# Transposing normalised activations on TensorE instead of by DMA, with part of a broadcast moved and the instruction order redone

## Chip, cores, metric

One core of a Trainium2 chip. The metric is the device time in microseconds of one execution. Several executions are taken in each job, and the kernel before runs beside every kernel that is tried, on the same chip. Engines are named as in the profile: PE (TensorE), PEld (its weight loads), DVE (VectorE), ACT (ScalarE), POOL (GpSimd), SP (the queue that issues DMAs).

## The reference

Four residual layers A, B, A, B on one sequence of 2048 tokens with 512 features and 32 heads of 16.

```
x = x + A(layernorm(x)); x = x + B(layernorm(x)); x = x + A(...); x = x + B(...)

A (linear attention):  q,k,v = x @ wqkv;  pq = q @ w_phi, pk = k @ w_phi  (per head)
    phi = [softmax(p), softmax(-p)]
    kv = sum over tokens phi_k v,  z = sum over tokens phi_k
    o  = (phi_q kv) / (phi_q z + 1e-6);  out = o @ wo

B (local attention):   8 keys at distance 0, 2, .., 14;  softmax(q k / 4);  out = (attn v) @ wo
```

Layer A sums over all keys before any query is answered. That is the one barrier in each pair of layers. The kernel works on four blocks of 512 tokens.

## The kernel before

The instruction stream of each engine follows a fixed list of steps (`_ORDER`, some 1,400 entries of two characters, made in advance). Each entry runs one step of one stage on one engine, and PE, DVE, ACT and SP keep the order in which the list emits them.

The norm makes `xn` on DVE, and one DMA per block transposes it, so that features lie on the partitions:

```python
def s_norm(self, st, key, b, T, op0, scale):
    # ... ln(): reciprocal standard deviation on ACT
    def ap(t):                       # DVE, four times 128 tokens
        if t == 0:
            T["xn"] = self.med([4, D], "xn")
        nc.vector.tensor_scalar(out=T["xn"][:, t, :], in0=self.x[b][:, t, :], ...)

    def tr():                        # SP
        xnT = self.med([4, NB, P], "xnT")
        nc.sync.dma_start_transpose(out=xnT[:].rearrange("k t c p -> k (t c) p"),
                                    in_=T["xn"][:].rearrange("p t d -> p (t d)"))
        self.xnT[key, b] = xnT
    add(st, "ACT", ln)
    for t in range(4):
        add(st, "DVE", ap, t)
    add(st, "SP", tr)
```

There are 16 such norms: four blocks ahead of each layer. In layer A the normaliser `rho` (one number for head and token) is spread over the features in one of two ways:

```python
# s_a3, after md (PE), dr (DVE), ln (ACT), rho (DVE)
for s in range(2):
    if dma:                          # blocks 1, 2, 3 of each layer
        add(st, "SP", wr, s)         # rho to DRAM
        add(st, "SP", rdb, s)        # read back 16-fold, 512 KB
        add(st, "DVE", muld, s)      # one product of 2048 columns
    else:                            # block 0
        add(st, "PE", bc, s)         # 16 small products with a 0/1 matrix, into four PSUM banks
        for t in range(4):
            add(st, "DVE", mulp, s, t)   # four products of 512 columns, from PSUM
```

Layer B writes V of a block to DRAM (`vd`) and reads it back shifted (`Vg`, 8 DMAs of 260 KB). DVE then multiplies queries with keys (`prod`) and weights with values (`pav`), in instructions of 2.3 us. At the start comes a check of the column norms of two folded weights.

At the start a check of the column norms of two folded weights squares them on POOL:

```python
def sq(qk):
    w = self.WA[:, :, qk * D:(qk + 1) * D]
    nc.gpsimd.tensor_tensor(out=T[qk][:], in0=w, in1=w, op=ALU.mult)
```

Of the kernel before, what the change touches and what calls it, by code (L numbers as in the profile page):

```python
# [8 lines left out]
BF16 = mybir.dt.bfloat16  # L9
# [3 lines left out]
ACT = mybir.ActivationFunctionType  # L13
# [10 lines left out]
NB = 4  # L24
# [11 lines left out]
SUM_R_MAX = 1e10  # L36
DEN_TINY = 2.0 ** -60

_OPT = {"rho_dma": (1, 2, 3), "pe_resid": {}}

_E = mybir.EngineType
_ORDERED = {_E.PE, _E.DVE, _E.Activation, _E.SP}
# [42 lines left out]


class _Fast:
# [97 lines left out]
    def setup(self):  # L185
        nc, const = self.nc, self.const
        nc.scalar.preload_act_table_set("natural_log_exp_and_others")
        self.WA = const.tile([P, NB, 3 * D], BF16, name="WA")
        self.WoA = const.tile([P, NB, D], BF16, name="WoA")
        self.WB = const.tile([P, NB, 3, NB, P], BF16, name="WB")  # L190
        self.WoB = const.tile([P, NB, D], BF16, name="WoB")
        WA = self.WA
        self.wraw = self.big([NB, 2 * D], "wraw")
        wraw = self.wraw
        wav = self.A_wqkv.rearrange("(m p) c -> p m c", p=P)
        self.phis = self.t2([NB, DH], "phis")
# [108 lines left out]
    def s_norm(self, st, key, b, T, op0, scale):  # L305
        nc, add = self.nc, self.step
# [13 lines left out]
        def tr():  # L320
# [514 lines left out]
    def stages(self):  # L835
        for b in range(4):
            self.s_ln_first(b)
        self.s_fold(1)
        self.s_fold(0)
        self.s_load_B()  # L840
        for L in range(2):
            for b in range(4):
                self.s_a1(L, b)
            for b in range(4):
                self.s_a2(L, b)
            if L == 0:
# [73 lines left out]
class _Layout:  # L920
# [578 lines left out]
```

## Time and profile before

| | before |
|---|---|
| time, median (3 runs) | 425.43 us |
| span in the trace | 422.1 us |
| PE / DVE / ACT busy | 327.1 / 317.0 / 253.6 us |
| DVE idle | 105.1 us |

A busy figure is the time in which the engine had an instruction in work. PE's includes the time that the half clock adds. The prediction shows the page's lines, and it cuts the span in three at the first of the six small DVE instructions that take the finished sums of a layer A (called ZM). I use the same cut, I, II and III, throughout. These are the rows of the windows table of the kernel before for the three (us; then busy time of PE, PEld, DVE, ACT, POOL; granted clock; DMA share; GB/s):

```profile
0.00:74.50 74.50, 50.24 (x378) 29.11 (x383) 48.85 (x93) 42.72 (x89) 17.11 (x33) 0.93 0.47 114
74.50:267.70 193.20, 167.04 (x1351) 75.26 (x1361) 148.44 (x224) 139.97 (x314) 0.83 (x5) 0.94 0.48 95
267.70:422.10 154.40, 109.81 (x778) 43.01 (x779) 119.70 (x159) 70.92 (x156) 0.15 (x1) 0.85 0.54 119
```

### The profile page before, as it was taken

The page shows a single profiled execution, that of the slowest core. Times are in us where ns is not written, and L with a number is a line of the kernel's source. Part 1 is how long each engine was busy: PE and PEld are TensorE (multiplying, and loading weights), DVE is VectorE, ACT ScalarE, POOL GpSimd, SP SyncE. Part 2 cuts the span into 40 slices and gives each one's busy share as a digit, 9 for nine tenths or more (in the row PEclk, how much of TensorE's full clock was granted, in tenths as well). Part 3 has the DMA queues.
Part 4 walks back from the last instruction along what each step waited for, and adds up shares of the span by engine and source line. Part 5 has one row for each costly group of instructions (what it writes and reads, how often), then busy time and mean ns, then how long its engine had stood idle before and what let it go on. Part 6 is the DMA issues. An engine that isn't in the chain of part 4 may idle for free.

```text
span 422.1 us, 6496 instructions
## 1 busy us (share of the span) xinstructions
PE 327.1 (78%) x2499; PEld 147.4 (35%) x2521; DVE 317.0 (75%) x476; ACT 253.6 (60%) x559; POOL 18.1 (4%) x39
## 2 busy tenths in 40 slices
PE   0449989889999948942999999519899999671582
PEld 0414438534444313410344364503344433120131
DVE  2796937868529999795679983546879999866893
ACT  1318798688767564680889978506797666630220
POOL 2334200000000000000000000000000000000000
PEclk9959999999999977995899999857999999975598
DMA  8966000244872991399202020084055018799913
GB/s 261 331 109 101 0 2 2 57 107 64 159 184 80 210 190 28 101 206 203 47 2 50 0 51 2 9 209 103 10 92 99 2 50 193 169 195 219 225 59 108
DMA packets 68166, 45.24 MB, mean 107 GB/s; under 512 B 38304, under 2 KB 66464, under 8 KB 68128
## 3 DMA queue, kind: packets, MB, share of 16 engines
q1 hardware_dynamic: 66544, 43.69, 48.5%
q10 hardware_dynamic: 1584, 1.07, 0.8%
q8 instruction: 21, 0.34, 0.4%
q14 instruction: 17, 0.14, 0.1%
HBM read 29.64 MB, written 6.72 MB: 86 GB/s over the span
## 4 chain that ended last, share of the span: by engine, by line
PE 41%; DMA 24%; DVE 19%; ACT 10%; issue 2%; SPq 1%; ACTq 0%; DVEq 0%
PE ps L676 16%; DMA xnT<-xn 5%; PE ps L506 5%; PE ps L363 5%; PE ps L423 4%; DMA vd<-V 4%; DMA Prho<-rd 4%; DMA Vg<-vd 3%; DMA rd<-rho 3%; DVE x L376 3%; PE ps L478 3%; DVE xn L317 3%; ACT Eq L512 2%; DMA wraw<-in_A_wqkv_dram 2%; PE ps L435 2%
## 5 line engine op out<-in xcount | busy, mean ns | idle before, releaser
L676 PE MATMUL ps<-xnT,WB 128*128 128x512 bf16 x384 | 87.6, 384 | 4.2 <-DMA xnT<-xn 4.1
L794 DVE TENSOR_TENSOR pav<-PT,Vg 128x4096 bf16<-128x4096 bf16 x32 | 71.9, 2287 | 17.7 <-DMA Vg<-vd 8.9
L734 DVE TENSOR_TENSOR prod<-QT,K 128x4096 bf16<-128x4096 bf16 x32 | 71.4, 2285 | 3.1 <-ACT QT L690 1.6
L676 PEld LDWEIGHTS <-WB 128*128 128x128 bf16 x384 | 37.0, 99 | 53.6 <-issue 10.5
L376 DVE SCALAR_TENSOR_TENSOR x<-ps,x 128x512 bf16<-128x512 f32 x64 | 42.9, 684 | 10.6 <-PE ps L363 10.5
L506 PE MATMUL ps<-xnT,WA 128*128 128x512 bf16 x128 | 31.9, 400 | 13.8 <-DMA xnT<-xn 13.2
L807 ACT CAST oT<-ps 128x512 bf16<-128x512 f32 x32 | 18.4, 590 | 40.2 <-PE ps L801 40.2
L512 ACT ACTIVATE Eq<-ps 128x512 bf16<-128x512 f32 x64 | 34.0, 625 | 13.4 <-PE ps L506 13.4
L801 PE MATMUL ps<-pav,indAV 128*32 128x512 bf16 x256 | 22.6, 449 | 23.9 <-DVE pav L794 23.5
L389 ACT ACTIVATE sqd<-x,nmean 128x512 bf16<-128x512 bf16 x48 | 34.4, 719 | 9.1 <-DVE nmean L382 8.8
L363 PEld LDWEIGHTS <-oT 128*128 128x128 bf16 x256 | 24.3, 101 | 39.7 <-issue 8.8
L435 PE MATMUL ps<-WA,xnT 128*128 128x512 bf16 x123 | 30.4, 391 | 9.8 <-DMA xnT<-xn 9.4
L429 ACT ACTIVATE Ek<-ps 128x512 bf16<-128x512 f32 x64 | 32.9, 636 | 2.6 <-PE ps L423 2.6
L363 PE MATMUL ps<-WoB,oT 128*128 128x512 bf16 x124 | 32.6, 408 | 1.1 <-ACT oT L807 0.8
L363 PE MATMUL ps<-WoA,oT 128*128 128x512 bf16 x123 | 30.1, 380 | 2.1 <-ACT oT L658 1.4
L423 PE MATMUL ps<-WA,xnT 128*128 128x512 bf16 x122 | 29.0, 379 | 0.7 <-DVE WA L241 0.4
L690 ACT CAST QT<-ps 128x512 bf16<-128x512 f32 x32 | 18.7, 586 | 13.4 <-PE ps L676 13.4
L658 ACT CAST oT<-ps 128x512 bf16<-128x512 f32 x32 | 16.8, 597 | 14.1 <-PE ps L652 14.1
L449 DVE TENSOR_TENSOR s<-Ek 128x2048 bf16<-128x2048 bf16 x8 | 12.8, 1600 | 16.5 <-ACT Ek L429 16.5
L506 PEld LDWEIGHTS <-WA 128*128 128x128 bf16 x128 | 12.8, 102 | 30.9 <-DMA xnT<-xn 13.8
L652 PE MATMUL ps<-Eq,R 128*128 128x512 bf16 x64 | 17.6, 414 | 7.0 <-DVE Eq L627 6.9
L627 DVE TENSOR_TENSOR Eq<-Eq,Prho 128x2048 bf16<-128x2048 bf16 x12 | 14.6, 1222 | 11.2 <-DMA Prho<-rd 11.2
(103 smaller groups left out, 391.4 us busy)
## 6 DMA issues: line engine op xcount, KB each, us to landing
Vg<-vd SPq DMA_DIRECT2D x64, 260.0 KB, 8.1
Prho<-rd SPq DMA_DIRECT2D x12, 512.0 KB, 4.8
vd<-V SPq DMA_DIRECT2D x8, 512.0 KB, 3.3
x<-in_A_x_dram SPq DMA_DIRECT2D x4, 512.0 KB, 9.8
out_dram<-x SPq DMA_DIRECT2D x8, 256.0 KB, 2.2
wbraw<-in_B_wqkv_dram SPq DMA_DIRECT2D x3, 512.0 KB, 10.0
wraw<-in_A_wqkv_dram SPq DMA_DIRECT2D x1, 512.0 KB, 4.3
WA<-in_A_wqkv_dram ACTq DMA_DIRECT2D x1, 512.0 KB, 7.5
```

Source lines behind the costliest of these rows:

```text
L363: nc.tensor.matmul(y[:], lhsT=oT[:, c, t * P:(t + 1) * P], rhs=Wo()[:, c, :], start=(c == 0), stop=(c == NB - 1 and t not in pe_res))
L376: nc.vector.scalar_tensor_tensor(out=xb[:, t, :], in0=T[t][:], scalar=1.0, in1=xb[:, t, :], op0=ALU.mult, op1=ALU.add, **kw)
L389: nc.scalar.activation(out=sqd[:], in_=xb[:, t, :], func=ACT.Square, bias=T["nm"][:, t:t + 1], accum_out=T["ss"][:, t:t + 1])
L423: nc.tensor.matmul(pk[:], lhsT=xnT[:, t, k, :], rhs=self.WA[:, k, D:2 * D], start=(k == 0), stop=(k == NB - 1))
L429: nc.scalar.activation(out=T["E"][:, t, s, :], in_=T["k", t][:], func=ACT.Exp, scale=1.0 - 2.0 * s)
L435: nc.tensor.matmul(pv[:], lhsT=xnT[:, t, k, :], rhs=self.WA[:, k, 2 * D:3 * D], start=(k == 0), stop=(k == NB - 1))
L506: nc.tensor.matmul(pq[:], lhsT=self.WA[:, k, hb * P:(hb + 1) * P], rhs=xnT[:, :, k, :], start=(k == 0), stop=(k == NB - 1))
L512: nc.scalar.activation(out=self.Eq[L, b][s][:, :, hb, :], in_=T[hb][:].rearrange("p (t i) -> p t i", t=4), func=ACT.Exp, scale=1.0 - 2.0 * s)
L676: nc.tensor.matmul(pp[:], lhsT=self.WB[:, k, i, c, :], rhs=xnT[:, :, k, :], start=(k == 0), stop=(k == NB - 1))
L734: nc.vector.tensor_tensor(out=pr[:], in0=QT[:, c:c + 1, :].to_broadcast([P, NW, TB]), in1=win, op=ALU.mult)
L794: nc.vector.tensor_tensor(out=pv[:], in0=PT[:].unsqueeze(1).to_broadcast([P, NB, 2, TB]), in1=vw, op=ALU.mult)
L801: nc.tensor.matmul(po[32 * c:32 * c + 32, :], lhsT=self.indAV[:], rhs=T["p", q][:, c, hf, :], start=(hf == 0), stop=(hf == 1), tile_positi ...
```

## The change

The intent: no norm waits for a DMA transpose any more; rho by DMA remains only for the blocks whose turn comes late; the first loads arrive in the order in which they are needed; and a new list orders the instructions around that.

```diff
-_OPT = {"rho_dma": (1, 2, 3), "pe_resid": {}}
+_OPT = {"rho_dma": ((0, 2), (0, 3), (1, 2), (1, 3)), "pe_resid": {}, "tr_dma": ()}
 _ORDER = """
 ... (all entries replaced: 1387 before, 1475 after)

# setup: everything but the small w_phi on SP's queue, in order of need
-        nc.sync.dma_start(out=wraw[:, :, D:2 * D], ...)         # K half
-        nc.sync.dma_start(out=self.x[0][:], ...)
-        nc.scalar.dma_start(out=WA[:, :, 2 * D:3 * D], ...)      # V part
-        nc.scalar.dma_start(out=wraw[:, :, 0:D], ...)            # Q half
-        for b in range(1, 4): nc.sync.dma_start(out=self.x[b][:], ...)
+        nc.sync.dma_start(out=wraw[:, :, D:2 * D], ...)
+        nc.sync.dma_start(out=self.x[0][:], ...)
+        nc.sync.dma_start(out=WA[:, :, 2 * D:3 * D], ...)
+        nc.sync.dma_start(out=self.x[1][:], ...)
+        nc.sync.dma_start(out=wraw[:, :, 0:D], ...)
+        for b in range(2, 4): nc.sync.dma_start(out=self.x[b][:], ...)

# s_norm
+        def pt(t):
+            if t % 2 == 0:
+                T["pt", t // 2] = self.ps(BF16)
+            for c in range(NB):
+                nc.tensor.transpose(T["pt", t // 2][:, ...], T["xn"][:, t, c * P:(c + 1) * P], self.ident[:])
+
+        def pe(h, copy):
+            ...
+            copy(out=self.xnT[key, b][:, 2 * h:2 * h + 2, :, :]..., in_=T["pt", h][:])
...
-        add(st, "SP", tr)
+            if (key, b) not in _OPT["tr_dma"]:
+                add(st, "PE", pt, t)
+                if t % 2:
+                    add(st, *(("ACT", pe, t // 2, nc.scalar.copy) if t == 1 else ("DVE", pe, t // 2, nc.vector.tensor_copy)))
+        if (key, b) in _OPT["tr_dma"]:
+            add(st, "SP", tr)

# rho: chosen by layer and block
-                self.s_a3(L, b, b in _OPT["rho_dma"])
+                self.s_a3(L, b, (L, b) in _OPT["rho_dma"])
```

The new list also takes the blocks in another order (layer 1: blocks 1 and 0 first, by PE broadcast, then 2 and 3 by DMA; before, 2 and 3 came first, by DMA). It mixes the projections of one block with the products of another, and it computes V of block 0 of layer 1 early.

More of the change, by code (lines that the diff above doesn't have):

```diff
@@ L46 @@
 _ORDER = """
-i i i f i c i g i 0 c i 3 i f e i 3 3 h f j j 3 j f f 3 h 0 f j 4 0 j h j 3 3 j 3 j 3 0 j 5 j 0 1 6 j 0 j 0 0
-0 6 2 6 6 t u 6 9 9 t 9 7 9 m n 6 6 6 m 6 9 8 d a m u g n 9 m 9 n 9 c 9 n c c d b e c t d e g k u 1k k l l k l
-l k l r l l 1k r l s o r s s r o s s o 10 s o 11 10 s 10 s p v 10 11 1i 11 v 11 1i v 1j v 1j 1i o w 1i 15 1j v
-15 1j 15 1j 1j 15 1j 1j 1i 16 16 y 1j y 16 z y z z y z z 1c z z 1c z 1c 16 12 16 1c 16 12 16 t 12 16 12 1d 17
-18 19 17 19 13 17 19 18 12 17 u 18 q 1d q 18 q 19 1d q 1a x 1d x 19 1d x 1d x 14 1d 14 1d 14 14 1b 1b 1b 1b 1n
@@ L52 @@
-1n 1c 1n 1n 1n 3y 1d 1n 1o 3z 40 1e 1p 3z 1q 1e 41 1f 1p 1e 1f 1f 1o 1f 1p 1o 1f 1p 1f 41 1p 1e 41 1p 1g 1f 1p
-1f 1p 2e 1h 1p 1h 1e 1p 41 1r 1f 1r 1s 2f 1r 1s 3z 1r 2g 1g 1s 2f 1s 1t 2h 1h 1h 1t 1u 1t 1u 1v 1u 3z 42 2h 2h
-1u 1u 1v 42 42 1u 43 42 1v 1t 43 1g 43 1u 2h 43 44 1u 1h 1h 44 45 1v 44 2f 1v 44 45 45 46 1g 45 45 46 45 1l 1h
-2f 46 2i 1h 45 36 2j 45 1u 46 2i 1u 1u 2i 46 1u 2i 2j 45 1w 1g 45 2j 45 2j 2k 45 1h 1m 2k 37 47 2l 2k 38 37 2k
-2l 2l 2m 39 1l 2l 2l 2m 1z 20 2l 2l 2l 1z 1m 2m 1z 39 2m 39 1z 2m 20 2l 4c 2l 20 2l 20 4c 2l 4d 2u 2n 4c 4d 4c
@@ L57 @@
-4d 37 21 39 4d 4f 21 22 21 22 2s 22 2s 2t 2s 2t 37 2s 2t 2q 2t 2v 2q 2r 2q 2r 2q 2r 2o 2r 3m 2o 2p 2w 2o 2p 2o
-2p 3a 2p 2w 3a 3b 3a 3b 3a 3b 21 3b 2w 1x 22 23 1x 1y 1x 1y 2w 1x 1y 48 1y 48 24 49 48 49 2v 48 2v 49 24 2v 25
-49 2v 2x 2v 2x 2v 2v 2x 24 2v 25 23 2x 2y 23 3c 23 2y 24 25 23 23 2x 23 3c 2y 23 3c 3d 23 2w 25 26 3d 3d 3c 3e
-3d 3d 4a 3e 3d 3d 4a 3e 3d 2z 3e 4a 3e 4a 4b 4b 3d 4b 30 3d 4b 3d 31 3d 2z 26 3f 24 30 2z 25 31 2z 26 3g 3g 3h
-24 27 3g 3h 3g 3h 27 3i 3h 3i 3j 27 3i 3j 3i 3j 3k 3j 27 3k 3l 3k 3l 3o 3k 3l 30 3l 30 3n 31 3o 28 31 3p 29 32
@@ L62 @@
-32 33 33 3p 33 34 32 33 3o 34 32 3n 3n 28 3n 28 29 33 3n 3p 29 3n 33 33 34 28 3n 33 3n 3o 29 2a 3n 34 2a 4f 34
-4f 2a 4f 33 4f 33 3p 33 4f 3q 33 2a 4f 2b 3q 35 3p 2b 2b 2c 2b 2b 3q 2b 2b 4f 2c 3o 4f 2c 2b 3r 2c 5k 2c 5k 5l
-2b 2b 5l 2b 3s 5l 2b 5k 5l 3r 2d 3t 5k 5l 5l 4x 5l 3r 5l 3s 4y 5k 3t 4x 4y 5l 3r 3s 4y 4q 3t 4y 4q 4r 4e 4g 4r
-3s 4r 4q 3t 4r 3u 4r 4g 3u 4r 3u 3u 3v 3v 4q 3v 3w 3v 3v 4x 3w 3v 3v 4r 4x 3w 3v 4g 5i 3w 5i 3w 4r 5i 4y 3v 4y
-3v 5i 3v 4y 3v 4y 4g 4h 3x 5j 4h 5j 4h 5j 5j 4z 50 51 4h 4i 4z 51 4i 51 4h 51 50 54 4u 4i 54 4u 55 54 55 4g 55
@@ L67 @@
-4j 54 55 55 5m 55 55 5m 4j 55 5n 5m 5n 5m 5n 5n 4j 4k 5n 4k 5n 5n 56 57 56 4j 5n 5m 52 4l 4k 5n 56 51 4l 4k 4l
-57 56 4l 4m 4u 57 4u 57 58 4m 4v 5j 4m 4n 5j 4n 4n 4m 5j 4o 4n 4n 4z 4o 4n 4n 4z 4o 4n 4u 4o 4s 4t 4s 4o 50 4s
-4n 50 4n 4w 4n 4t 4n 4s 4t 58 4p 5j 4w 58 4t 4w 58 4w 59 53 58 53 53 53 5i 5j 5a 5b 5b 5c 5c 5b 5c 5c 5b 5c 5c
-5o 5c 5c 5o 5p 5f 5o 5p 5p 5o 5f 5p 5f 5p 5d 5e 5f 5d 5g 5d 5p 5f 5p 5d 5p 5o 5e 5e 5a 5p 5a 5e 5a 5h 5h 5h 5h
-5q 5q 5q 77 5q 5q 7y 78 5r 5q 79 7z 6g 78 80 5s 7a 7z 5t 6h 81 6i 7a 7a 81 81 7a 5s 5r 81 6h 5r 5s 6j 78 7z 5s
@@ L72 @@
-6j 78 7b 6j 7z 7b 7c 7c 7b 5s 7b 7c 5s 6j 82 5s 7c 5s 82 83 5s 82 5s 83 6h 5u 83 5u 5v 5u 5v 5u 5v 82 6h 5v 5w
-83 5w 5x 5w 5x 5x 5y 5w 5x 5x 5y 6k 5x 5x 5y 6k 6k 5x 6l 6k 6l 7d 6l 6l 6m 7e 5y 6m 7e 6n 5y 7f 6m 5x 5x 5x 6m
-5x 6n 6n 5z 6o 7d 6n 6n 6o 7d 6n 6n 6o 7d 6n 7e 6o 84 7e 7e 6o 7f 84 6n 6n 6n 62 63 6n 85 62 6p 85 85 86 62 85
-63 7e 7e 62 86 7e 63 84 63 84 85 7f 6w 85 7f 60 85 86 6s 85 86 6s 86 7f 6s 85 61 85 6t 85 6s 85 6t 7e 6t 87 6q
-7e 6t 7e 7e 6q 6r 7n 67 6q 6r 7g 6q 6r 6y 6u 6r 68 6v 8a 6y 8a 8b 7j 8b 7j 7k 6y 7j 7k 7j 7k 8a 6y 7k 8a 8b 88
@@ L77 @@
-8b 8e 88 89 8g 88 89 88 89 7l 89 8g 7l 7m 7l 7m 8g 7l 7m 6z 7m 6z 7o 6z 8g 6z 70 7h 70 6z 7i 7h 70 7p 7h 7i 7h
-7i 6y 7q 7i 7p 6u 6u 6v 6u 6v 7p 7q 6v 60 6x 60 61 7p 7q 61 60 8c 61 67 7q 8d 7r 8c 7o 7r 7q 7o 67 8d 7o 68 7r
-7o 8c 7o 7o 8c 8d 7p 7o 67 68 7o 8d 8h 8f 8h 8h 7s 68 69 8h 69 64 8i 7s 64 8i 65 7t 65 8f 8h 7u 8f 64 7s 8i 8f
-7t 8f 8f 64 7u 8f 65 8g 8f 65 7t 8f 7s 7u 66 67 7t 8j 68 7u 7v 69 8j 7v 6x 6x 6x 7w 7v 6x 7w 6x 7v 6x 7w 7x 67
-8k 6x 7w 8k 6x 8l 8j 7x 8l 66 66 66 66 71 8k 66 8l 66 66 66 71 72 73 71 72 73 71 72 73 8j 72 73 74 6a 8k 74 8l
@@ L82 @@
-6a 8m 6a 8m 8m 8n 8m 8n 6b 8n 8o 6b 6c 8n 6b 6c 6a 8o 74 6c 74 75 6b 75 6c 6d 75 76 6d 6e 75 6d 6e 76 6d 6e 6f
-6e 6f
+i i c i i c d i i e c 0 i i 0 c i c e 0 c e 0 0 1 d 0 0 2 0 2 0 3 2 1 2 3 m n 0 3 f 3 f m 6 h 6 m 4 n 6 m n 6
+n 6 3 3 7 6 5 6 8 6 8 6 7 8 3 8 3 5 6 5 4 10 11 3 j 9 j 5 10 3 j 9 10 j 11 j 9 10 j 11 9 j t 11 9 u g j t j d
+a j k 9 u j 9 k 9 l j 9 l k l l k l l y l l y z o y z z y o z o z f o f z f f g p b b g z b b o r z h r h s 1c
+1k s 9 q s 12 q s q 1d q 12 1d 1c a 12 12 1c 1k 1d 13 15 1d 12 15 1d 16 15 16 16 15 16 16 1c 16 16 1l 16 1l 1d
@@ new lines @@
+19 1d r 1d 19 1c 19 s 19 s r 1m 1a 1g 1m 1d 19 s 1g s 1h 1g 1h 1g 1h v 1h 17 18 v 17 v v 1h 17 18 w 17 18 v t
+1h 18 t u 1h 1i u 1h x 1j x x 1j x 1g 14 1h 14 14 14 1b 1b 1b 1b 1n 1n 1i 1n 1n 1n 31 1j 1n 1j 1o 32 33 1i 1p
+32 1q 1i 34 1j 1p 1e 1j 1j 1o 1j 3r 1p 1f 1p 34 1o 1f 34 1p 1i 1p 1p 1e 1j 1p 1e 1f 3s 1f 1p 1e 3t 1p 1f 1r 3s
+1f 1r 1s 3u 32 1r 34 1s 1r 1s 1s 1t 1f 1t 1u 1f 3u 1u 1t 3u 1u 1v 1u 1t 1u 1v 1u 2c 1u 1v 1u 1e 32 1v 35 1v 1f
+1u 35 1u 36 35 1u 36 1u 35 1t 3s 36 3u 1t 1t 36 1t 1v 37 1u 2d 37 38 2e 1w 38 38 39 1w 38 1x 2d 2c 39 1w 2d 1x
@@ new lines @@
+3s 2c 1x 1w 2d 2d 1x 3v 2d 3w 3v 3v 2d 3w 3v 3w 2d 37 3w 2d 37 38 38 1y 1z 38 38 2d 1y 39 23 1y 1z 39 1y 1z 3x
+1z 23 24 39 3x 3x 3y 24 3y 3y 3z 3x 3y 3y 3z 20 3y 3y 3z 20 3y 23 3z 20 3z 21 20 21 3y 21 24 3y 21 3y 3x 3x 3y
+22 3x 3z 23 2f 3x 2f 2g 2f 2g 2f 2g 3y 2g 2h 38 2h 2i 22 2h 2i 22 2i 2j 22 2h 2i 2i 22 2j 22 24 2i 2i 2j 22 22
+40 2i 25 38 22 38 25 40 38 2j 2q 23 40 2j 41 24 2i 2i 40 41 2i 25 2i 2h 2h 2h 2h 2j 23 42 2i 42 41 41 26 2k 43
+43 2k 2l 2k 26 2l 2k 2l 2m 2l 26 2m 2n 2m 2n 2m 2n 2s 42 2n 42 43 3g 2s 2t 43 44 44 45 2s 2t 45 44 44 45 2s 2t
@@ new lines @@
+45 37 37 47 37 39 37 27 38 2t 28 26 3c 2u 2u 3c 3d 3c 3d 3c 3d 3a 3d 46 3a 48 3b 3a 3b 3a 3b 3i 2t 3b 3e 2u 3e
+48 3f 3e 3f 3e 3f 3j 3i 3f 49 3h 49 27 48 27 28 3j 28 27 2o 28 3i 47 29 2p 47 47 29 47 47 29 2a 47 2a 29 47 2a
+2b 47 2a 2a 3j 2b 49 2a 2a 2b 2o 2a 48 2b 2o 2b 2p 2o 2p 2a 49 2p 2a 4a 2a 29 2r 29 2a 29 4a 49 3i 2b 29 4a 4h
+2a 4h 4i 48 4i 59 3h 4b 4i 3h 59 4i 3h 5a 59 3h 5a 3h 5a 4b 59 3h 5a 3h 5a 4h 3h 5a 5a 4h 5a 4b 59 4i 4i 3j 5a
+4c 4i 2r 2s 4i 4c 2r 4b 4d 2r 4c 4d 2r 4j 4k 2r 2r 4j 2r 4d 4l 4c 2r 3k 4j 4d 4l 3k 4e 4l 4k 4l 4e 4k 4f 4m 4f
@@ new lines @@
+4e 4f 4g 4f 4e 4f 4g 4f 4l 3j 4g 4j 3k 4k 4f 4n 4n 4f 2v 4g 4n 4n 4g 4f 2w 4f 4f 4e 2x 4e 4f 4e 4g 2v 4e 52 52
+53 4f 53 2w 2v 53 52 53 2x 52 53 53 54 55 2v 2w 53 54 53 3i 2w 55 3l 54 2x 2x 2y 55 2y 2z 2y 2z 2z 30 2y 2z 2z
+30 3m 2z 2z 30 54 2z 3n 3l 30 5f 30 5f 5g 5g 2z 5f 2z 5g 2z 2y 5g 2z 2y 2y 5g 3l 2y 30 3m 3n 5f 5g 2z 55 4o 5g
+3l 3m 4p 4p 4o 3n 4o 4p 56 4p 3m 4p 4o 3n 56 4p 3o 56 4p 56 4p 3o 3p 5g 3o 3p 57 3p 3q 3o 3p 3p 3q 5f 3p 3p 3q
+3p 5b 5g 56 3q 5b 3q 5b 5c 5c 3p 5b 3p 5c 3p 5c 3o 3p 3o 4s 5c 3o 3o 3q 4q 4r 3p 4v 4s 5c 4v 4s 4w 4s 4w 4v 4t
@@ new lines @@
+4w 4v 4s 4w 4q 4w 4w 4q 4w 4w 4u 4r 4q 4z 4r 4u 5c 4z 4u 4r 5c 5b 4z 4z 4u 50 4x 4y 4z 4x 5c 4x 4y 4x 4y 51 4y
+51 51 51 58 58 58 58 5h 5h 5d 5h 5h 5h 66 5e 5h 5e 5i 67 68 7l 5j 67 5k 5d 7m 66 5j 5e 67 66 5e 67 7n 5d 67 67
+5d 5e 67 5e 5i 67 5e 5e 67 6v 67 69 5j 69 6a 5j 5i 6a 5j 69 5j 69 6a 5j 5d 6a 5j 6b 5e 5j 6b 6w 6c 6b 6x 6c 6c
+6d 6b 6c 6c 6d 6c 6c 6d 6c 6w 6d 5j 5l 6y 6d 7m 6c 5l 7o 5m 6c 5l 5m 6c 6b 6c 6b 5m 6b 6d 6b 6y 5l 6c 6y 5m 5n
+7o 7o 5n 5o 5n 5o 5p 5o 5n 5o 5p 5o 6e 5o 5p 5o 6e 5o 5p 6w 6y 6e 5p 6f 5o 6e 5o 6f 5o 6f 5o 5n 6f 5n 5n 5p 7m
@@ new lines @@
+5n 7o 6g 5o 6g 6h 5s 5t 5s 6w 6h 5s 5t 5s 5t 6g 5t 7m 6g 6h 6k 6m 6z 6h 6z 70 6z 70 6z 70 5u 7a 6m 70 71 5v 71
+72 71 72 72 73 71 72 72 73 5u 72 72 73 5u 72 5v 6m 5u 73 73 5q 5v 5v 72 5q 72 5r 5w 72 71 5r 71 5x 71 73 5q 5q
+5r 5x 6n 5r 5y 5w 6n 5w 6n 5w 5x 5y 5w 5w 7p 5w 7p 7q 7p 5w 7q 7p 5w 5x 7q 5y 7q 7r 7r 72 5y 6m 5z 7r 5z 7r 71
+5x 7s 5y 72 6n 5z 7s 6i 7s 74 7t 7s 5x 7t 7s 74 75 7s 7s 74 7t 7s 60 74 7t 7t 76 75 75 76 77 7s 7s 75 7r 7c 77
+7r 76 7t 76 77 78 7c 6o 77 7d 79 78 6o 6j 80 7d 7c 79 78 78 79 7c 7d 79 61 7b 6n 62 6i 6o 7s 7d 7s 60 7r 7e 7r
@@ L84 @@
+6i 7e 6j 7d 6j 6i 6m 7e 7s 61 60 62 7u 6j 7u 7v 6l 7u 7v 7c 7u 60 7v 7w 7v 7w 7x 6l 82 7w 7x 6l 6l 7w 7x 6l 6l
+61 7x 82 6l 83 62 6l 61 6l 7y 62 7b 7b 82 63 7z 7b 7b 83 7b 63 7b 82 7b 83 7b 63 63 6p 83 84 7y 84 83 7z 6p 7y
+84 6q 7z 7y 6r 82 7z 6q 6p 81 6r 7f 6q 6r 7f 7g 7h 7f 7g 81 81 81 7h 81 7f 81 7g 81 81 7h 81 6p 7g 7h 7i 64 85
+7i 7i 7j 7j 7i 7j 7k 86 7j 6q 87 85 7k 6r 6s 6s 6s 85 86 6s 87 85 86 87 64 86 64 65 87 88 64 88 89 65 6t 88 89
+88 89 8a 6t 89 6u 6t 8a 6t 6u
 """
@@ L196, in setup @@
         self.phis = self.t2([NB, DH], "phis")
-        nc.sync.dma_start(out=wraw[:, :, D:2 * D], in_=wav[:, :, D:2 * D])
+        xv = self.A_x.rearrange("b (j p) d -> p (b j) d", p=P)
+        self.x = [const.tile([P, 4, D], BF16, name="x%d" % b) for b in range(4)]
         with nc.allow_non_contiguous_dma(reason="tiny w_phi load"):
             nc.scalar.dma_start(out=self.phis[:], in_=self.A_w_phi.rearrange("(hb hl) d f -> (hl d) hb f", hb=NB))
-        xv = self.A_x.rearrange("b (j p) d -> p (b j) d", p=P)
-        self.x = [const.tile([P, 4, D], BF16, name="x%d" % b) for b in range(4)]
+        nc.sync.dma_start(out=wraw[:, :, D:2 * D], in_=wav[:, :, D:2 * D])
         nc.sync.dma_start(out=self.x[0][:], in_=xv[:, 0:4, :])
-        nc.scalar.dma_start(out=WA[:, :, 2 * D:3 * D], in_=wav[:, :, 2 * D:3 * D])
-        nc.scalar.dma_start(out=wraw[:, :, 0:D], in_=wav[:, :, 0:D])
-        for b in range(1, 4):
+        nc.sync.dma_start(out=WA[:, :, 2 * D:3 * D], in_=wav[:, :, 2 * D:3 * D])
+        nc.sync.dma_start(out=self.x[1][:], in_=xv[:, 4:8, :])
+        nc.sync.dma_start(out=wraw[:, :, 0:D], in_=wav[:, :, 0:D])
+        for b in range(2, 4):
             nc.sync.dma_start(out=self.x[b][:], in_=xv[:, 4 * b:4 * b + 4, :])
@@ L324, in tr @@
             self.xnT[key, b] = xnT
+        def pt(t):
+            if t % 2 == 0:
+                T["pt", t // 2] = self.ps(BF16)
+            for c in range(NB):
+                nc.tensor.transpose(T["pt", t // 2][:, (t % 2 * NB + c) * P:(t % 2 * NB + c + 1) * P],
+                                    T["xn"][:, t, c * P:(c + 1) * P], self.ident[:])
+        def pe(h, copy):
+            if (key, b) not in self.xnT:
+                self.xnT[key, b] = self.med([4, NB, P], "xnT")
+            copy(out=self.xnT[key, b][:, 2 * h:2 * h + 2, :, :].rearrange("p t c i -> p (t c i)"),
+                 in_=T["pt", h][:])
         add(st, "ACT", ln)
```

## The prediction

> **What bounds the kernel now.** I read the page first: busy shares and the slices.
>
> ```profile
> PE 327.1 (78%) x2499; PEld 147.4 (35%) x2521; DVE 317.0 (75%) x476; ACT 253.6 (60%) x559; POOL 18.1 (4%) x39
> ...
> PE   0449989889999948942999999519899999671582
> ...
> DVE  2796937868529999795679983546879999866893
> ...
> PEclk9959999999999977995899999857999999975598
> DMA  8966000244872991399202020084055018799913
> ...
> PE 41%; DMA 24%; DVE 19%; ACT 10%; issue 2%; SPq 1%; ACTq 0%; DVEq 0%
> ```
>
> No engine is full over the whole span. Where the PE digits fall (start, slices 15, 18-19, 26-27, end) the DMA digits rise and the granted clock drops. A quarter of the chain that ended last is DMA. So: PE and DVE are near saturation in between, and a few DMA round trips cost the rest. The chain in order of time names them, and the table by windows, cut at those places, gives their size (columns: us, then busy time of PE, PEld, DVE, ACT, POOL, then granted clock, DMA share, GB/s).
>
> ```profile
> 151.52 8.32 DMA xnT<-xn
> ...
> 188.18 10.04 DMA xnT<-xn
> ...
> 278.16 6.25 DMA Prho<-rd
> ...
> 356.56 8.87 DMA vd<-V
> ...
> 392.68 10.13 DMA Vg<-vd
> ```
>
> ```profile
> 0.00:27.00 27.00, 4.76 (x48) 4.33 (x48) 16.24 (x47) 5.18 (x9) 9.77 (x29) 0.86 0.91 256
> ...
> 185.00:198.00 13.00, 0.07 (x1) 0.00 (x0) 10.47 (x17) 4.39 (x13) 0.00 (x0) 0.70 1.16 200
> 198.00:267.70 69.70, 68.34 (x569) 32.80 (x577) 49.62 (x63) 58.97 (x131) 0.51 (x3) 0.96 0.16 31
> 267.70:300.00 32.30, 17.10 (x217) 8.08 (x214) 21.08 (x45) 11.98 (x27) 0.15 (x1) 0.74 0.43 105
> ...
> 357.00:403.00 46.00, 25.88 (x174) 7.69 (x169) 35.81 (x27) 13.90 (x30) 0.00 (x0) 0.70 0.95 195
> ```
>
> PE is idle 22 us before 27, 5 us at 152.5-160 (same cause as the next), 13 us at 185-198, 15 us at 267.7-300 and 20 us at 357-403. Between these it is busy 92 to 99%. At 185-198 a transpose by DMA takes 10.0 us beside a 1.16-full DMA (the reads of V by 64 issues of 260 KB); the median of the 16 is 4.7. At 267.7-300 every block of layer 1 but one waits for rho written to DRAM and read back. I divide the span at the two places where the sums over keys are complete (the first ZM instruction, 74.5 and 267.7): phases I of 74.5, II of 193.2 and III of 154.4 us, with PE busy 50.2, 167.0, 109.8 and DVE busy 48.9, 148.4, 119.7.
>
> **The Trainium skill.** "DMA: Bandwidth & Descriptors", Issuing engines are not separate DMA queues: all issuing engines share the same 16 DMA engines and interleave. The trace agrees: the same transpose takes 4.2 us at best and 10.0 beside the V reads, and the Q half of the folded weight, issued from ACT's queue beside SP's loads, landed 9.9 us after issue against 4.3 for the K half. "TensorE: Matmul & The Clock Gate", Part 1, HAM oscillation: PE gaps above about 3.4 us bring the half clock back. The trace agrees: granted clock 0.52 to 0.74 around the gaps, 1.00 in the dense stretches. Same page, Part 4, PE-mode transpose: a full 128x128 transpose to PSUM that needs an eviction, about 275 ns in one kernel, and it says that transposes do not count as activity for the clock. The trace has 32 such transposes of wraw at 313 ns each, overlapped; below.
>
> **The change part by part.**
>
> ```profile
> 11.89 3.60 PE L228 MATMUL ps<-ident,wraw 128*128 128x128 bf16 x32 [11.89 <-DMA wraw<-in_A_wqkv_dram]
> ...
> 67.16 7.36 PE ps L478 x123
> ...
> L232 ACT COPY wT<-ps 128x1024 bf16<-128x1024 bf16 x2 | 1.9, 1014 | 12.6 <-PE ps L228 12.6
> L232 DVE COPY wT<-ps 128x1024 bf16<-128x1024 bf16 x2 | 1.4, 688 | 6.9 <-PE ps L228 6.9
> L607 DVE TENSOR_TENSOR Eq<-ps,Eq 128x512 bf16<-128x512 f32 x16 | 9.9, 682 | 0.5 <-PE ps L601 0.5
> L627 DVE TENSOR_TENSOR Eq<-Eq,Prho 128x2048 bf16<-128x2048 bf16 x12 | 14.6, 1222 | 11.2 <-DMA Prho<-rd 11.2
> ```
>
> Removed: 16 DMA transposes (four blocks at each of four norms) and 4 of 12 rho reads (block 1 of each layer, two halves each). Added for the norms: 16 x 16 = 256 transposes with as many weight loads. A warm weight load and 128-column product pair costs 7.36/123 = 60 ns in the kv products; the wraw transposes, right after idle, cost 3.60/32 = 112 ns. I take 60: 15 us of PE (29 if they stay at 112). Each norm adds one copy of 128x1024 on ACT and one on DVE: 16 x 1.01 = 16 us ACT, 16 x 0.69 = 11 us DVE. Block 1 by PE broadcast: two blocks x 8 x 0.682 = 10.9 us of DVE for two x 2 x 1.222 = 4.9 removed, so +6; PE +2. Sums: PE 327 + 17 = 344, DVE 334, ACT 270, less what the half clock had put into PE. So no gain comes from less work: the change adds work and must earn it by closing gaps.
>
> Phase I. Before, the first weight transposes wait for the Q half (11.89) and the first V product for the DMA transpose (27.0); then PE needs 47.5 us to 74.5. Now the K half is loaded first and its fold comes first: it should land near 5.5 (issue 1.3 plus 4.3), DVE's first copy at about 7.5 instead of 12.96, the first normalised block at 14, transposed and evicted by 16. Then 47.5 + 64 x 0.06 = 3.8 + 1.7 for the column check (moved here) ends at 69. Gain 5.5; the rest of the 11 us head start is PE work that was there anyway. DVE cannot take the bound: its own sum to this point is 49 + 3 us from 7.5, so 60.
>
> Phase II is PE's. 167 busy, of which about 5 is half clock; 162 + 128 transposes at 0.06 (7.7) + 1.1 for block 1's broadcast - 3.5 (most of one Q projection is now after the boundary) - 1.7 (column check) = 166. At 95% dense (before: 92 to 99% outside the gaps) 174, against 193.2: gain 19. DVE's floor here is 148.4 + 5.5 + 3 = 157, ACT's 140 + 8, so both have room.
>
> Phase III is DVE's: 119.7 + 4 x 0.69 + 3 = 125.5. Add 6 us for the latency of the first rho (sums, reciprocal, broadcast; now two blocks go by PE while the two DMA ones travel), 5 of scattered stalls, 6.6 from DVE's last instruction (415.5) to the end as before: 143, against 154.4. Gain 11. The V projections are now spread over the phase (block 0's right after its K), so the V round trips that fill 357-403 begin earlier, under the products.
>
> Sum 5.5 + 19 + 11 = 35.5: span 387, and with the 3.3 us between span and time, 390 us.
>
> **The rivals.** (a) *DVE takes the bound.* 334 of 387 us is 86%; at 130-170 DVE is already full while PE waits in part of it. If DVE also fills phase II (157 at 92% = 171) nothing much changes; if PE and DVE starve each other, since copies to free PSUM sit in the order between 2.3 us products, II takes 185 and the time is 402. (b) *Transposes stay at 112 ns.* 192 of them in I and II at 52 ns more is 10 us of PE on the path: 400. Against: after 3.4 us of work the fold products fell to 56-68 ns each; for: the skill's note. (c) *The gaps are really DVE's or the V reads'.* In 152.5-160 and 185-198 DVE is 99% and 81% busy, so without the transpose DVE's own queue could delay PE; and the last block's V write and read stay. Then only 5 + 10 + 5 is won: 405. (d) *Better than summed*: with PE never cold and the tail hidden, PE's warm 324 plus about 45 for start and end gives 372.
>
> **Range and chances.** Middle 390; (a) to (c) pull to 400-405, (d) to 375. Range 377 to 406. To miss 2% (417) the gain would have to be under a quarter of the idle that the DMA transposes and rho reads alone open; the new order is a whole new schedule, so I leave 5% for it: faster 0.95, same 0.04, slower 0.01.
>
> **What would show it.** Right: no transpose rows in the DMA issues and 8 rho reads; first V product near 16; first ZM at 69 and at about 243; PE digits 9 where 15, 18-19 and 26-27 were low; transposes about 60 ns apart, copies at 1.01 and 0.69 us; in phase III DVE over 85% and DMA off the chain but for the last block. Wrong: a PE wait for DVE or ACT copies of xnT of the same size as the DMA waits; transposes 107 ns apart; granted clock still near 0.7 at the end; the first ZM later than 72.

## More of the kernel before

One execution of the kernel before, among 11 in one job, took 1156 us where the others took 423 to 426; it is in no ratio, and it stays unexplained, since there is no trace of it.

## The result, and the profile after

394.34 us median of 4 runs (392.94 to 396.30) against 425.75. The ratio is 0.9265, 95% interval 0.9216 to 0.9314. A ratio here is the mean time of one kernel's fast runs over that of the other's of the same rounds, so it is not quite the ratio of the medians quoted.

The page after, the lines that answer to those of before:

```profile
PE 342.2 (87%) x2841; PEld 161.4 (41%) x2841; DVE 335.7 (86%) x504; ACT 268.2 (69%) x575; POOL 19.6 (5%) x39
...
PE   3789959998999999988869999987999999973871
...
DVE  6986968387999797998999997498979999998893
...
PEclk9989989999999999999999999999999999995798
...
PE 38%; DVE 22%; ACT 20%; DMA 14%; issue 2%; SPq 1%; DVEq 0%; ACTq 0%
```

Every engine does more: PE +15.1 us, DVE +18.7, ACT +14.6. The span is 30.9 us shorter because idle time went: DVE idled 105.1 us before and 55.5 now, 49.6 less, of which 18.7 is spent on the added work. The low digits in the middle of PE's row are gone, and so are the low granted clocks; the fall near the end is still there. The three phases after, from the windows table:

```profile
0.00:76.20 76.20, 61.91 (x491) 35.64 (x492) 56.18 (x101) 48.94 (x97) 18.58 (x33) 0.96 0.29 84
76.20:251.80 175.60, 165.82 (x1432) 78.21 (x1430) 155.13 (x235) 140.60 (x308) 0.83 (x5) 1.00 0.35 74
251.80:391.20 139.40, 114.46 (x926) 47.51 (x923) 124.39 (x169) 78.67 (x170) 0.15 (x1) 0.94 0.48 109
```

| phase | before | predicted gain | after | measured gain | DVE idle before, after |
|---|---|---|---|---|---|
| I | 74.5 | 5.5 | 76.2 | -1.7 | 25.7, 20.0 |
| II | 193.2 | 19 | 175.6 | 17.6 | 44.8, 20.5 |
| III | 154.4 | 11 | 139.4 | 15.0 | 34.7, 15.0 |

And the rows of the added work: the groups of instructions (busy us, mean ns; then the engine's idle time before them), and one block's transposes from the chain (start, length):

```profile
L333 PE MATMUL ps<-ident,xn 128*128 128x128 bf16 x256 | 20.4, 229 | 3.6 <-DVE xn L320 3.6
L628 DVE TENSOR_TENSOR Eq<-ps,Eq 128x512 bf16<-128x512 f32 x32 | 19.7, 679 | 1.1 <-PE ps L622 1.1
L339 ACT COPY xnT<-ps 128x1024 bf16<-128x1024 bf16 x16 | 16.5, 1033 | 5.1 <-PE ps L333 5.1
L339 DVE COPY xnT<-ps 128x1024 bf16<-128x1024 bf16 x16 | 10.9, 681 | 1.3 <-PE ps L333 1.3
```

```profile
131.29 0.89 PE ps L333 x16
```

0.89/16 is 56 ns from one transpose to the next. A single one shows 229 ns, but they overlap. The first block's 16, right after idle, started 107 ns apart. The copies cost 1.03 and 0.68 us each. The spacing and the copies were priced right; PE's busy time for all 256 is 20.4 us, where 15 were reckoned.

### The profile page after: what moved, and what is told of

The parts are those of the page before. It is cut to its first block, busy times and chain, and to the rows that moved or that the text cites. A ratio compares the mean times of both kernels' runs of the same rounds, so it can differ in the third digit from the quotient of the medians.

```text
span 391.2 us, 7145 instructions
## 1 busy us (share of the span) xinstructions
PE 342.2 (87%) x2841; PEld 161.4 (41%) x2841; DVE 335.7 (86%) x504; ACT 268.2 (69%) x575; POOL 19.6 (5%) x39
## 4 chain that ended last, share of the span: by engine, by line
PE 38%; DVE 22%; ACT 20%; DMA 14%; issue 2%; SPq 1%; DVEq 0%; ACTq 0%
PE ps L697 14%; DMA Vg<-vd 11%; PE ps L456 5%; PE ps L384 5%; ACT Ek L450 4%; DVE pav L815 4%; DVE x L397 4%; DVE prod L755 4%; ACT sqd L410 4%; ACT Eq L533 3%; PE ps L527 3%; PE ps L499 3%; DVE Eq L628 2%; DMA vd<-V 2%; PE ps L762 2%
## 5 line engine op out<-in xcount | busy, mean ns | idle before, releaser
L828 ACT CAST oT<-ps 128x512 bf16<-128x512 f32 x32 | 18.5, 590 | 27.9 <-PE ps L822 27.9
L444 PE MATMUL ps<-WA,xnT 128*128 128x512 bf16 x128 | 30.5, 384 | 5.8 <-ACT Eq L533 4.5
L822 PE MATMUL ps<-pav,indAV 128*32 128x512 bf16 x256 | 21.0, 412 | 15.5 <-DVE pav L815 15.5
L456 PE MATMUL ps<-WA,xnT 128*128 128x512 bf16 x128 | 31.9, 394 | 0.3 <-ACT xnT L339 0.3
L384 PE MATMUL ps<-WoB,oT 128*128 128x512 bf16 x128 | 31.2, 394 | 0.0
L463 ACT CAST vaug<-ps 128x512 bf16<-128x512 f32 x32 | 18.6, 599 | 7.5 <-PE ps L456 7.5
L711 ACT CAST K<-ps 128x512 bf16<-128x512 f32 x32 | 18.5, 593 | 7.5 <-PE ps L697 7.3
L333 PE MATMUL ps<-ident,xn 128*128 128x128 bf16 x256 | 20.4, 229 | 3.6 <-DVE xn L320 3.6
L490 DVE TENSOR_TENSOR Ek<-Ek,rk 128x4096 bf16<-128x4096 bf16 x8 | 18.3, 2287 | 4.6 <-ACT rk L487 4.6
L333 PEld LDWEIGHTS <-xn 128*128 128x128 bf16 x256 | 16.5, 102 | 11.6 <-DVE xn L320 7.8
L711 ACT CAST V<-ps 128x512 bf16<-128x512 f32 x32 | 17.9, 594 | 4.8 <-PE ps L697 4.6
```

What stands on the lines that cost most here:

```text
L333: nc.tensor.transpose(T["pt", t // 2][:, (t % 2 * NB + c) * P:(t % 2 * NB + c + 1) * P], T["xn"][:, t, c * P:(c + 1) * P], self.ident[:])
L384: nc.tensor.matmul(y[:], lhsT=oT[:, c, t * P:(t + 1) * P], rhs=Wo()[:, c, :], start=(c == 0), stop=(c == NB - 1 and t not in pe_res))
L456: nc.tensor.matmul(pv[:], lhsT=xnT[:, t, k, :], rhs=self.WA[:, k, 2 * D:3 * D], start=(k == 0), stop=(k == NB - 1))
L711: nc.scalar.copy(out=dst, in_=T[i, c][:])
```

## The experiments

An edit of the changed kernel keeps the new list: a step that is taken out leaves its place empty, and what replaces it is issued from that place. An edit of the kernel before keeps the old list in the same way. So "new order" and "old order" below are the lists as they are. All results were correct unless it says otherwise.

### Undo one part in the new order

**Transposes back on DMA.**

```diff
         def pt(t):
+            if t == 3:
+                tr()          # the DMA transpose, where the last PE transpose stood
+            return
         def pe(h, copy):
+            return            # no copies
```

> The changed kernel with all 16 transposes given back to the DMA, in the changed order (the DMA transpose is issued where the last PE transpose of a block stood; its copies are left out). Theory (the gain is the wait for the DMA transposes): a DMA transpose takes 4.2 to 10 us where 16 transposes and a copy take about 2, so 2 to 6 us at most of the 16 norms come back: 415 to 440 us, with PE waiting for DMA at the first product after each norm. Rival 1 (the gain is the order and the rho): within 8 us of the changed kernel, 387 to 402. Rival 2 (the copies on ACT and DVE cost as much as they save): faster than 394.

459.6 us, 65 above the changed kernel and 1.081 times the kernel before. This is beyond even the theory's range. The waits in its trace (us in total, times, longest):

```profile
PE ps L703 <- DMA xnT<-xn: 25.6, 8, 6.8
...
PE ps L462 <- DMA xnT<-xn: 22.7, 2, 15.6
...
PE ps L450 <- DMA xnT<-xn: 17.4, 4, 5.4
```

66 us of PE waits for the transposes in 14 places. The new list puts the first product right behind the norm, where a transpose on PE is ready in about 2 us. Part of one wait is SP's queue and not the transpose: the first block was normalised at 12.0 us, and its transpose was issued at 18.5, behind the loads. So the new order needs the PE transposes. It does not follow that the transposes alone brought 65 us, or 31; see below.

**Block 1's rho back on DMA.**

```diff
-        def bc(s): ...  def mulp(s, t): ...       # PE broadcast, products from PSUM
+        bc(s)  ->  wr(s); rdb(s)                  # for block 1 of both layers
+        mulp(s, 0)  ->  muld(s);  mulp(s, 1..3) -> nothing
```

> The changed kernel with block 1 of both layers back on the DMA broadcast of rho, in the changed order. Theory (the DMA round trip of about 11 us per block held PE at 267.7-300 before): 6 to 14 us slower, 400 to 408, nearly all of it after the second ZM (layer 1). Rival (DVE is the bound of that phase, so 6 us less DVE work pays for the wait): 391 to 397.

413.66 us, 19 slower; more than I expected, and in both layers: phase II is 184.1 (+8.5) and phase III 151.5 (+12.1), although DVE has 2.4 and 2.1 us less to do in them. The line of the wait:

```profile
DVE Eq L648 <- DMA Prho<-rd: 18.8, 5, 6.5
```

The theory holds, and its "nearly all in layer 1" does not. In layer 0 DVE waits for these reads too: 6.5 and 2.2 us of the 18.8, at 109 to 114 us.

**Loads as before.**

```diff
-        nc.sync.dma_start(out=WA[:, :, 2 * D:3 * D], ...)   # and the Q half
+        nc.scalar.dma_start(out=WA[:, :, 2 * D:3 * D], ...)
```

> The changed kernel with the loads issued as before (V and Q weights from the ACT queue, beside the first x block). Theory: the first block of x and the V weight land later by sharing the DMA engines, so the first V product comes 2 to 4 us later, but the first ZM later by less than 2: 394 to 397. Rival (the start sets the end): 3 to 5 us slower, 397 to 400.

394.34 us, the same as the changed kernel. The queue and order of the loads are worth nothing measurable here. The first V product came at 14.0 us instead of 13.5, not 2 to 4 us later. The first ZM came at 77.9 instead of 76.2, but runs of the changed kernel itself differ by that much (78.4 in a second trace).

### One part, or all, in the old order

**PE transposes alone, and all three parts.**

```diff
 # kernel before, s_norm: in place of tr(), at its place in the list
+        def tr_pe():   # 16 transposes into two PSUM banks, one copy on ACT, one on DVE
-        add(st, "SP", tr)
+        add(st, "SP", tr_pe)
 # for the second kernel also: rho of block 1 by PE, and the new loads
```

> The kernel before with PE transposes alone, at the place where the DMA transposes were issued, in the old order, rho and loads as before. If the old order gains nothing from the removed waits: 423 to 430, as with all three parts (427.8). If the rho by PE or the new loads spoiled that run: 408 to 420.

> The kernel before, in its own order, with all three parts of the change put in (PE transposes and both copies at the place where the DMA transpose was issued, rho of block 1 by PE, new load queue). Theory (the removed waits make the gain): 400 to 412. Rival (the new order makes it; old order merely exchanges DMA waits for PE and copy waits): 415 to 428. In the old order the Q half of the weight is folded first, and the new queue loads it last: the start should be a few us worse than either.

427.13 us (ratio 1.0049, interval 1.001 to 1.0089) and 427.80 us (1.0071, interval 1.0032 to 1.0111). In the old order the same instructions gain nothing; both intervals lie just above 1. The theory of the second expectation, 400 to 412, fell. (In that run block 1's broadcast and its products are issued together, at the old place of its product.)

**No transposes at all, in both orders.** Wrong results: the products read `xn` untransposed, of the same shape.

```diff
-            nc.sync.dma_start_transpose(out=xnT..., in_=T["xn"]...)      # old order
-            (pt, pe of the changed kernel: left out)                      # new order
+            self.xnT[key, b] = T["xn"][:].rearrange("p t (c i) -> p t c i", i=P)
```

> Wrong result on purpose: the kernel before, its own order, with the DMA transposes left out (the products read the normalised block as it is, same shape and size); nothing put in their place. It measures what all waits for DMA transposes are worth in the old order, free of charge. If the waits were on the path as the prediction summed them (27 us in at the start, 7.5 at 152, 13 at 185): 385 to 400. If DVE, 99% and 81% busy in those windows, and the V reads at the end keep the end where it is: 412 to 424. After the old-order run I lean to the second.

> Wrong result on purpose: the changed kernel with the PE transposes and their 32 copies left out, products on the block as it is. It measures what the transposes cost where they stand: 15 us PE, 16.5 ACT, 10.9 DVE of work. If PE and DVE share the bound nearly everywhere: 10 to 16 us less, 378 to 384. If they lie in slack: within 4 us of the changed kernel.

Old order 410.79 us (ratio 0.9663), new order 385.99 us (0.9112). Both fell between the two branches of what was expected. They tell two things apart.

First, with every transpose wait taken away for nothing, the old order wins only some 14 us. Phase I stays at exactly 74.5, although the first V product started at 20.6 instead of 27.0. Phase II falls to 180.5, phase III to 152.9. The windows table of that kernel over the two places of phase II where PE had waited for transposes:

```profile
152.50:160.00 7.50, 5.29 (x30) 2.27 (x30) 7.41 (x6) 4.95 (x11) 0.00 (x0) 1.00 0.75 137
185.00:198.00 13.00, 9.47 (x93) 3.64 (x94) 12.85 (x17) 12.87 (x32) 0.17 (x1) 1.00 0.57 105
```

DVE is 99% busy in both. In the first it was 99% busy before too, and little was won there. In the second it had been 81% busy, and most of the gain lies there. Both kernels run the same list, so I compare the start of the same DVE instruction in both traces. The one without transposes is 1.0 us behind at 169.9 us of the kernel before, 0.9 ahead at 174.8, 8.3 at 202.9 and 12.6 at 227.6. In the kernel before, PE waits for the transpose, and right behind that DVE waits for PE:

```profile
198.27 1.04 PE L506 MATMUL ps<-xnT,WA 128*128 128x512 bf16 x2 [13.20 <-DMA xnT<-xn]
```

```profile
202.90 2.29 DVE L794 TENSOR_TENSOR pav<-PT,Vg 128x4096 bf16<-128x4096 bf16 x1 [7.34 <-PE ps L801]
```

Without transposes that product runs with the two before it in one row, and DVE does not wait:

```profile
190.17 6.69 DVE L791 TENSOR_TENSOR pav<-PT,Vg 128x4096 bf16<-128x4096 bf16 x3
```

So of PE's three waits for transposes, 9.4 us (to 27.0), 4.1 (to 159.9) and 13.2 (to 198.3), the first was worth nothing, the second at most 1.8 us and the third nearly 12.

Second, the transposes with their copies cost about 8 us in the new order (394.3 against 386.0) but 16 in the old one (427.1 against 410.8). In the traces it is 4.6, 9.7 and 6.2 us of the phases I, II and III, 20 in all; the trace with PE transposes is of its slowest run. That kernel closes the third wait too: matched in the same way, it is 9.9 us behind the kernel before at 193.3 us, 0.5 ahead at 212.8, and 6.3 behind at the end. Taking 14 and giving 16 back is the whole result of the transposes in the old order.

**Why rho by PE brought nothing in the old order.** In its layer 1 the old list takes blocks 2 and 3 first, by DMA, so block 1 was not the one that PE waited for. One edit gives PE broadcast to those two:

```diff
-  (1, 2), (1, 3): wr, rdb on SP, muld on DVE
+  (1, 2), (1, 3): bc on PE and mulp on DVE, issued where wr stood
```

> The kernel before with one edit in layer 1: of the four blocks, those that its order takes first (2 and 3) get rho by PE broadcast, block 1 stays on DMA; layer 0 and the DMA transposes as before. It asks why rho of block 1 by PE gained nothing in the old order. Theory (only the block that PE takes next matters, and in the old order that is block 2, by DMA): the 17 us at 267.7-300 in which PE is idle shrink by 8 or more, time 414 to 419. Rival (number of DMA blocks matters, or the tail takes it back since DVE or the V reads set the end): 421 to 427.

422.50 us (0.9969, interval 0.9934 to 1.0005): the rival. (A first form, issued where `muld` stood, deadlocked over PSUM banks in the simulator and never ran.) The windows table, 268 to 298:

```profile
268.00:278.00 10.00, 4.69 (x188) 3.45 (x188) 9.85 (x25) 2.84 (x8) 0.00 (x0) 0.73 0.01 3
278.00:288.00 10.00, 5.11 (x58) 2.61 (x58) 9.64 (x18) 2.22 (x5) 0.15 (x1) 0.59 0.14 40
288.00:298.00 10.00, 8.72 (x40) 3.65 (x39) 5.17 (x11) 5.25 (x11) 0.00 (x0) 1.00 0.29 74
```

Up to 288 us the DMA wait is gone, and DVE, multiplying from PSUM, is 97% busy for 20 us in its place. PE still idles for half of them. Behind that DVE still waits 4.7 us for the rho of block 1, which stays on DMA. Phase III gains only 2 us (152.4), and its last part looks as before, with the V transfers in it. In the old order, then, removing this wait turned most of it into DVE work.

### The start: squares on POOL

Phase I missed its prediction. The timelines of DVE and POOL in the changed kernel show two additions of DVE that take 4.0 us where their sisters take 1.22 and 0.69, beside the squares:

```profile
42.48 4.02 DVE L470 TENSOR_TENSOR s<-Ek 128x2048 bf16<-128x2048 bf16 x1
46.53 3.97 DVE L474 TENSOR_TENSOR s<-s 128x1024 bf16<-128x1024 bf16 x1
```

```profile
41.53 8.42 POOL L290 TENSOR_TENSOR sq<-WA 128x2048 bf16<-128x2048 bf16 x2 [16.91 <-ACT WA L244]
```

The Trainium skill, page "SBUF — State Buffer", section Who interferes with whom, says that a DVE instruction with two SBUF inputs contends with a GpSimd instruction that reads SBUF, over ports that it calls an exclusive lock. Both additions have two inputs in SBUF, and each ends 0.5 to 1.1 us after one of the two squares. The kernel before has the same hold-up, but only one addition falls beside its squares (37.16 to 44.3 us):

```profile
41.15 4.25 DVE L449 TENSOR_TENSOR s<-Ek 128x2048 bf16<-128x2048 bf16 x1 [4.14 <-ACT Ek L429]
```

It lost 3.0 us there, so the new order doubled a loss that its trace already showed. The test moves the squares to DVE:

```diff
-            nc.gpsimd.tensor_tensor(out=T[qk][:], in0=w, in1=w, op=ALU.mult)
+            nc.vector.tensor_tensor(out=T[qk][:], in0=w, in1=w, op=ALU.mult)
```

> The changed kernel with the two squares of the column check on DVE instead of GpSimd. Theory (GpSimd's two squares of 4.2 us at 41.5 to 49.9 hold up two DVE additions, 4.0 us each instead of 1.22 and 0.69, and PE and ACT then wait): DVE loses 2.4 us of work and wins 6.1, so the first ZM comes 3 to 5 us earlier, and the time is 389.5 to 392. Rival (PE's sum bounds this phase anyway, or later phases absorb it): 393 to 396.

> The changed kernel once more, as the companion on one chip of the two runs that follow: 393 to 396.

> The changed kernel with the squares on DVE, on the same chip as the changed kernel. Theory (GpSimd's squares hold up DVE; first ZM came 5.5 us earlier in its trace): 3 to 5 us under its companion. Rival (the difference to the earlier run of the changed kernel was the chip): within 1.5 us of it.

First job: 390.38 us (0.9198, interval 0.9166 to 0.923). Second job, with the changed kernel on the same chip: 390.38 (0.9209, interval 0.9179 to 0.9239) against 393.95 (0.9291, interval 0.9265 to 0.9316). So it is 3.6 us faster, and faster than both kernels of the case. The same two additions in its timeline:

```profile
43.37 1.22 DVE L470 TENSOR_TENSOR s<-Ek 128x2048 bf16<-128x2048 bf16 x1
44.62 0.69 DVE L474 TENSOR_TENSOR s<-s 128x1024 bf16<-128x1024 bf16 x1
```

The first ZM came at 70.7 and 71.2 us instead of 76.2 and 78.4. Of these 5.5 and 7.2 us the medians keep 3.6; the two pairs of traces are of runs that lie apart from their medians by up to 3 us, so what becomes of the rest is open.

**Both copies on ACT for the norms ahead of layer B**, on top of that:

```diff
+            if key[0] == "B":
+                copy = nc.scalar.copy
             copy(out=self.xnT[key, b][:, 2 * h:2 * h + 2, :, :]..., in_=T["pt", h][:])
```

> The last one, and for the eight norms ahead of the B layers both copies of the transposed block on ACT: DVE loses 8 x 0.68 = 5.4 us, ACT gains 8 x 1.03 = 8.3. If DVE is what sets the pace of the B stages now: 2 to 5 us less than the squares on DVE alone. If the second copy, behind the first on the same engine, makes PE wait (1 us for each norm): 0 to 6 us more.

394.25 us, 3.9 slower than the squares on DVE alone. Less DVE work did not help; the second branch of the expectation holds. That it is the second copy's wait on the same engine was argued, not isolated.

## Why the prediction was right, and where not

The time, 390 predicted and 394.3 measured, is the sum of three phases. Against the prediction phase I is 7.2 us longer, phase II 1.6 longer and phase III 3.6 shorter, so III hid half of what I missed; that part is luck. The prediction earned its gain by closing PE's gaps at DMA waits. The runs show that this alone does not earn it: the same edits in the old list gain nothing.

- **The work added** (PE +17, ACT +16, DVE +17 with the rest): right in size, +15.1, +14.6 and +18.7. Transposes 56 ns apart (60 taken; rival (b), 112, is out: only the first 16 of the span, after idle, and some of the third block were 107 ns apart), copies 1.03 and 0.68 us, PE broadcast 0.68 us a product. The 256 transposes hold PE for 20.4 us and not 15. With them left out, the new order's PE is busy 323.9 us, so they add 18.3, and the rest of the change takes 3 off. Some 3 us of DVE's rise are the hold-up by POOL below.
- **Phase II, "166 us of PE at 95% dense":** measured 165.8 busy in 175.6, 94%. The size is right. The reason given, that the two PE gaps at transposes were on the path, holds for one of them: 185 to 198 was worth nearly 12 us, 152.5 to 160 at most 1.8. Without any transpose the old order has a phase II of 180.5, 12.7 shorter; with PE transposes it has 190.2. The new order does it in 175.6 with them. What the trace shows of the difference is DVE's work being spread: at 110 to 130 us the kernel before had DVE at 3.06 and 4.89 of 10 us, and then full for long stretches; the changed kernel has 9.86 and 8.40 there. Rival (c), that the gaps are DVE's, was nearly right about the first gap of the old order and wrong about the second, where DVE waited for PE. That the spread of DVE's work is what brings the rest is argued, not isolated. The prediction called the order "a whole new schedule" and gave it only a chance of harm, not a share of the gain.
- **Phase III, "DVE's 125.5 plus stalls, 143":** DVE measured 124.4, stalls 15.0 instead of 17.6, and 139.4 in all. The rho part is shown in the new order (12.1 us back when block 1 goes by DMA). That V is spread over the phase is in the order, and no run isolates it. DMA is still on the chain that ended last (14%), but DVE was busy 41.8 of the 45 us from 340 to 385, so these V reads cost DVE at most 3 us, and not what their share suggests.
- **Phase I, gain 5.5:** failed, -1.7. The head start came as predicted, even sooner (first V product at 13.5, predicted 16). Two steps were wrong. "The first V product at 27.0; then PE needs 47.5 us" took the wait at 27 for the start of the path; with it removed in the old order the phase stays 74.5 us, since the K fold waits in DVE's queue behind the norms (DVE's copy for it starts at 32.6 us in both traces, and PE, now earlier, waits 5.1 us for it). And "DVE cannot take the bound" added only the 3 us of copies to DVE's sum and nothing for a hold-up by POOL, where the two additions lost 6.1 us (2.8 and 3.3; the kernel before lost 3.0 in one), with ACT waiting 5.8 us and PE 4.5 behind them. With the squares on DVE the phase takes 70.7 and 71.2, about 2 from the 69 predicted.
- **The load order** was part of the head start in my working. Its worth is 0 within the runs' scatter.

Open: which feature of the new list carries the gain (the mixing of projections and products, the order of blocks, V of block 0 early). The runs show that the list without the PE transposes loses 65 us, that the transposes without the list lose about 2, and that together they win 31. The parts cannot be given shares.

## What to carry to other kernels

The length of a PE gap behind a DMA does not tell what closing it is worth: here waits of 9.4, 4.1 and 13.2 us were worth nothing, at most 1.8 and nearly 12. DVE's busy share in the same window is a hint and no more, since its own wait for PE can come just behind (7.3 us here, though it was 81% busy beside the gap). Take the wait out with a deliberately wrong kernel, which costs one run, and compare the start of the same instruction in both traces. When a fixed order is tuned around a latency, swapping the slow operation alone may gain nothing, and a new order without the swap may lose much; judge the pair. And where one instruction shows three times the time of its sisters, look at what the neighbouring engine ran beside it.

## What the Trainium skill lacked or had wrong

- "TensorE: Matmul & The Clock Gate", Part 4, PE-mode transpose: it gives about 275 ns for one in a kernel and no spacing; the page has a spacing only elsewhere, for plain products. Here one transpose shows 229 ns on average, and 16 in a row start 56 ns apart (0.89 us), weight loads included, so the single duration is four times the spacing. It says that transposes do not count as activity for the clock; with 128 of the 256 mixed into the products of phase II the granted clock was 1.00 there, so no loss by it shows here, and a long run of transposes alone was not tried.
- "SBUF — State Buffer", Who interferes with whom: the trace agrees, with sizes for this pair that it does not give: a 0.69 us addition took 3.97 beside a GpSimd square of 4.6 us. What the page lacks is the cost further on: moving the two squares to DVE made the kernel 3.6 us faster although it gave DVE 2.4 us more to do.
- "DMA: Bandwidth & Descriptors", Issuing engines are not separate DMA queues: the runs agree. Loads on two queues or one (the order changed with it) gave 394.34 us each.
- No page says how to tell which of PE's waits for a DMA are worth closing: taking every transpose out of the old order won 14 us, where PE had waited 26.7 us for them (9.4, 4.1 and 13.2), and most of the gain came from the last.
